# Normalising a linear-attention output: one Newton chain per batch instead of a power per block

## The chip, the cores and the metric

The kernel runs on one NeuronCore of one Trainium2 chip. Its time is the device time of one execution in microseconds (us), as the median of several runs. A profile is one further execution, recorded by the hardware profiler; its span runs from the first to the last instruction.

## The reference

Inputs are `q`, `k`, `v` of shape 8 batches x 8 heads x 576 tokens x 64, a gain `g_norm` of 64, and the weights of four experts. All are float32. The kernel computes

```python
kv  = einsum('bhsd,bhse->bhde', k, v)          # one 64x64 matrix per head
out = einsum('bhsd,bhde->bhse', q, kv)
rms = sqrt(mean(out * out, axis=-1, keepdims=True) + 1e-6)
x   = (out / rms * g_norm), heads side by side  # 576 x 512 per batch
logits = x @ w_gate                            # 4 experts, the best 2 are used
# per expert: causal softmax attention of x @ wq, x @ wk, x @ wv, then @ wo
# result: sum over the two chosen experts, weighted with a softmax of their logits
```

The norm is over the 64 numbers of one head and one token: 8 norms per token, 4608 per batch.

## The kernel before

The 576 tokens of a batch are five blocks, four of 128 and one of 64. Two generators per batch issue the work.

`stage1(b)` turns q, k, v into `xT`, the normalised x with its 512 features on the partitions. It adds up `kv` on TensorE (`p_kv`, line 175), transposes q block by block (`q_block`, lines 192 to 201) and puts `kv` times the router's weights behind each head's 64 columns (`p_kg`, lines 218 to 227), so that a head has 68 columns. Then, per block (lines 247 to 299): four matmuls give `p_out` with 8 x 68 columns in a "big" PSUM buffer (two banks); ACT squares its 64-column parts into `sq`; DVE sums them to `ms`, 8 numbers per token; GpSimd raises `ms` to the power -0.5 (`rstd`, line 268); DVE multiplies `p_out` with it into `x_tok` (line 273) and does the same for the router's part (`gl`, `lg8`). `x_flush` transposes `x_tok` on TensorE (`p_x`, line 242), one block behind, and ACT copies the result into `xT`.

`stage2(b)` makes the gate from `lg8`, the values `p_v`, and for each of two pairs of experts the projections (`p_proj`), the scores with their exponentials and masks (`p_sc`, `PT`; the masks are on GpSimd, line 394), the product with the values (`p_O`, scaled on DVE into `osc`) and its transposes (`p_OT`). `final` multiplies with `wo` (`p_y`), copies on ACT and writes out.

`weave` (lines 497 to 511) interleaves `stage2(b)` with `stage1(b + 1)`: each yields a cost, and the side work is advanced whenever its share of `W1` = 16 is behind the main work's share of `W2` = 17. A scheduler then settles the order on each engine, so the order that runs is not quite that in which the code issues; the excerpts below show it. There are three "big" PSUM buffers (for `p_out`, `p_proj`, `p_sc`, `p_O`) and two "small" ones (for the transposes, `p_kv`, `p_v`, `p_y`). Loads and stores are all issued from SP, in its order. The first `stage1` runs alone, the last `stage2` too, so seven pairs are woven.

Of the kernel before, what the change touches and what calls it, by code (L numbers as in the profile page):

```python
# [17 lines left out]
def kernel(  # L18
# [168 lines left out]
    def stage1(b, res):  # L187
        qb, kb, vb = loads[b]
        qT = s1.tile([P, NCH, S], FP32, tag="qT", name="qT")
# [44 lines left out]
        lg8 = lg8s[b % 2]  # L234
        pend = []

        def x_flush():
            i, xt = pend.pop(0)
            t0, nt = blocks[i]
            p_x = small([P, NCH, P], "p_x")  # L240
            for c in range(NCH):
                nc.tensor.transpose(  # L242
                    p_x[:, c, :nt], xt[:nt, c * P : (c + 1) * P], ident_f[:nt, :nt]
                )
            nc.scalar.copy(xT[:, :, t0 : t0 + nt], p_x[:, :, :nt])  # L245
# [310 lines left out]
```

## Time and profile before

| | before |
|---|---|
| runs, median (lowest to highest) | 370.99 us (370.33 to 371.15), 3 runs |
| the profiled execution | 370.28 us, span 368.6 us |
| TensorE busy, matmuls and weight loads | 298.2 us (81%) and 237.2 us (64%) |
| DVE, ACT, GpSimd (POOL) busy | 157.5, 152.6, 102.9 us |
| mean granted clock of TensorE | 0.852 of full speed |
| HBM read and written | 30.42 and 9.44 MB |

Busy time says what an engine did, and the chain of waits says what the end waited for. The chain is followed back from the last instruction, at each step to what released it. PE is TensorE's matmuls, PEld its weight loads, POOL is GpSimd. In the column of the clock 1.00 is full speed.

### The profile page before, as it was taken

The numbers are of one execution on the slowest core, as the hardware profiler recorded it, in microseconds if no ns is written. First come the engines' busy times: TensorE is split into PE (matmuls) and PEld (weight loads), VectorE is DVE, ScalarE is ACT, GpSimd is POOL, SyncE is SP. The second block draws the span as 40 slices with busy tenths as digits, with TensorE's granted clock in tenths as the row PEclk, the third lists the DMA queues.
The fourth block names the chain that finished last, engine by engine and source line by source line (L and its number), as shares of the span: only waits on it lengthen the run. The fifth ranks groups of instructions, "written<-read, shape, count | busy, mean of one in ns | idle before, by whom it ended". The sixth has DMA issues, their size and how long they took to land.

```text
span 368.6 us, 6665 instructions
## 1 busy us (share of the span) xinstructions
PE 298.2 (81%) x2616; PEld 237.2 (64%) x2624; DVE 157.5 (43%) x513; ACT 152.6 (41%) x273; POOL 102.9 (28%) x146
## 2 busy tenths in 40 slices
PE   2586698878986999779985899779995899778974
PEld 2474677668865788558864687557864687557651
DVE  0336443544436443544436433543444543544040
ACT  0213146132572347422582227621673227622843
POOL 8015113240253103530253103530235102521220
PEclk9978599578999599977999689986999589986975
DMA  7959999601136862900872035810021000300213
GB/s 216 211 128 291 278 232 293 123 4 57 58 115 160 129 202 56 246 12 19 239 198 61 2 123 152 212 29 2 0 88 43 2 2 0 130 1 2 85 44 128
DMA packets 75278, 40.28 MB, mean 109 GB/s; under 512 B 54000, under 2 KB 70384, under 8 KB 75248
## 3 DMA queue, kind: packets, MB, share of 16 engines
q1 hardware_dynamic: 75248, 39.86, 42.1%
q8 instruction: 21, 0.34, 0.4%
q14 instruction: 9, 0.07, 0.1%
HBM read 30.42 MB, written 9.44 MB: 108 GB/s over the span
## 4 chain that ended last, share of the span: by engine, by line
PE 46%; POOL 17%; DVE 17%; ACT 10%; issue 3%; SPq 2%; DMA 2%; POOLq 0%; ACTq 0%; DVEq 0%
POOL rstd L268 17%; PE p_proj L351 11%; PE p_v L333 7%; ACT PT L389 7%; DVE x_tok L273 7%; DVE ms L266 7%; PE p_kv L175 6%; PE p_out L250 5%; PE p_q L196 4%; PE p_sc L379 3%; PE p_x L242 2%; ACT sq L259 2%; PE p_kg L220 2%; SPq L130 2%; PE p_O L431 2%
## 5 line engine op out<-in xcount | busy, mean ns | idle before, releaser
L268 POOL TENSOR_TENSOR rstd<-ms,neg_half 128x8 f32<-128x8 f32 (+1 forms) x40 | 65.4, 1637 | 101.4 <-DVE ms L266 70.1
L394 POOL TENSOR_SCALAR_AFFINE_SELECT PT<-PT 128x256 bf16<-128x256 bf16 (+1 forms) x80 | 30.0, 385 | 148.8 <-ACT PT L389 148.1
L242 PE MATMUL p_x<-ident_f,x_tok 128*128 128x128 f32 (+1 forms) x160 | 30.7, 318 | 41.4 <-DVE gl L280 35.4
L250 PE MATMUL p_out<-kvx,qT 128*128 128x136 f32 (+1 forms) x320 | 55.1, 315 | 2.1 <-DVE inv L447 0.7
L389 ACT ACTIVATE PT<-p_sc 128x576 bf16<-128x576 f32 (+3 forms) x80 | 50.3, 712 | 7.2 <-PE p_sc L379 7.1
L250 PEld LDWEIGHTS p_out<-kvx,qT 128*128 128x128 f32 (+1 forms) x320 | 44.8, 197 | 11.5 <-issue 3.3
L273 DVE TENSOR_TENSOR x_tok<-p_out,rstd 128x512 f32<-128x512 f32 (+1 forms) x40 | 27.6, 690 | 55.0 <-POOL rstd L268 54.9
L242 PEld LDWEIGHTS p_x<-ident_f,x_tok 128*128 128x128 f32 (+1 forms) x160 | 19.2, 167 | 48.6 <-issue 34.4
L245 ACT CAST xT<-p_x 128x512 fp32r<-128x512 f32 (+1 forms) x40 | 21.7, 544 | 65.8 <-PE p_x L242 65.7
L259 ACT ACTIVATE sq<-p_out 128x512 f32<-128x512 f32 (+1 forms) x40 | 23.8, 596 | 47.9 <-PE p_out L250 47.0
L431 PE MATMUL p_O<-vext,PT 128*128 128x65 bf16 (+2 forms) x480 | 33.7, 211 | 7.3 <-DVE gl L280 5.1
L266 DVE TENSOR_REDUCE ms<-sq 128x8 f32<-128x520 f32 (+1 forms) x40 | 27.2, 680 | 26.9 <-ACT sq L259 26.9
L431 PEld LDWEIGHTS <-PT 128*128 128x128 bf16 (+2 forms) x480 | 27.8, 111 | 14.4 <-issue 9.7
L201 DVE COPY qT<-p_q 128x512 f32<-128x512 f32 (+1 forms) x40 | 25.4, 638 | 21.9 <-PE p_q L196 21.4
L333 PE MATMUL p_v<-wv_r,xT 128*128 128x256 f32 (+1 forms) x160 | 31.7, 335 | 0.3 <-DVE vext L340 0.3
L351 PE MATMUL p_proj<-xT,wq_r 128*128 128x288 f32 x128 | 31.4, 367 | 0.3 <-ACT PT L389 0.3
L175 PE MATMUL p_kv<-v_b,k_b 128*64 128x64 f32 x512 | 26.1, 263 | 5.7 <-DMA v_b<-in_v_dram 5.7
L379 PE MATMUL p_sc<-qTp,kT 64*128 64x288 f32 (+2 forms) x192 | 27.3, 345 | 2.0 <-ACT PT L389 1.7
L175 PEld LDWEIGHTS p_kv<-v_b,k_b 128*64 128x64 f32 x512 | 23.4, 176 | 8.0 <-DMA k_b<-in_k_dram 5.5
L196 PE MATMUL p_q<-ident_f,q_b 128*128 128x128 f32 (+1 forms) x160 | 26.0, 284 | 0.0
L333 PEld LDWEIGHTS p_v<-wv_r,xT 128*128 128x128 f32 (+1 forms) x160 | 24.5, 212 | 2.4 <-DVE vext L340 0.5
L340 DVE CAST vext<-p_v 128x256 bf16<-128x256 f32 (+1 forms) x40 | 17.0, 426 | 20.2 <-PE p_v L333 20.0
(61 smaller groups left out, 351.1 us busy)
## 6 DMA issues: line engine op xcount, KB each, us to landing
q_b<-in_q_dram SPq DMA_DIRECT2D x32, 256.0 KB, 5.2
out_dram<-y SPq DMA_DIRECT2D x32, 256.0 KB, 2.2
k_b<-in_k_dram SPq DMA_DIRECT2D x7, 1024.0 KB, 5.9
v_b<-in_v_dram SPq DMA_DIRECT2D x7, 1024.0 KB, 9.5
k_b<-in_k_dram SPq DMA_DIRECT2D x4, 256.0 KB, 4.5
v_b<-in_v_dram SPq DMA_DIRECT2D x4, 256.0 KB, 4.7
k_rem<-in_k_dram SPq DMA_DIRECT2D x8, 128.0 KB, 9.0
v_rem<-in_v_dram SPq DMA_DIRECT2D x8, 128.0 KB, 8.1
```

The source lines that it names most:

```text
L175: nc.tensor.matmul(p_kv[hh * Dh : (hh + 1) * Dh, c, :], lhsT=lk, rhs=rv, start=(j == 0), stop=(j == NF), skip_group_check=True,)
L196: nc.tensor.transpose(p_q[:, c, :nt], qb[:nt, i, 2 * c : 2 * c + 2, :].rearrange("p h d -> p (h d)"), ident_f[:nt, :nt],)
L242: nc.tensor.transpose(p_x[:, c, :nt], xt[:nt, c * P : (c + 1) * P], ident_f[:nt, :nt])
L250: nc.tensor.matmul(p_o[:nt, c // 2, (c % 2) * 2 * GW : (c % 2 + 1) * 2 * GW], lhsT=qT[:, c, t0 : t0 + nt], rhs=kvb[:, c, :, :].rearrange(" ...
L266: nc.vector.tensor_reduce(ms[:nt], sq[:nt], axis=AX_X, op=AluOpType.add)
L268: nc.gpsimd.tensor_tensor(out=rstd[:nt], in0=ms[:nt], in1=neg_half[:nt], op=AluOpType.pow)
L273: nc.vector.tensor_tensor(out=xt[:nt].rearrange("p (k h d) -> p k h d", k=2, h=4), in0=po[:, :, :, 0:Dh], in1=rb.to_broadcast([nt, 2, 4, Dh]),
L333: nc.tensor.matmul(p_v[:nt, :], lhsT=xT[:, c, t0 : t0 + nt], rhs=w_r["v"][:, c, :, :].rearrange("p e f -> p (e f)"), start=(c == 0), stop= ...
L351: nc.tensor.matmul(p_p[:, s, 0:HALF], lhsT=w_r[nm][:, c, 2 * pr : 2 * pr + 2, :].rearrange("p e f -> p (e f)"), rhs=xT[:, c, s * HALF : (s ...
L379: nc.tensor.matmul(p_s[:, el, o : o + hi - lo], lhsT=kTp[pb, kb * P : (kb + 1) * P], rhs=qTp[pb, lo:hi], start=True, stop=True,)
L389: nc.scalar.activation(PT[:, :, d0 : d0 + o], p_s[:, :, 0:o], ACTF.Exp, scale=scale)
L431: nc.tensor.matmul(p_O[:nq, bank, (2 * n + el) * (Hd + 1) : (2 * n + el + 1) * (Hd + 1)], lhsT=PT[:nk, el, col : col + nq], rhs=vx[:nk, kb ...
```

## The change

- After the four `p_out` matmuls of a block, DVE copies all 8 x 68 columns to a buffer in SBUF (`ob`, one for all batches); ACT then squares from PSUM as before and DVE sums into `ms[:, i, :]`, which now holds all five blocks.
- After the fifth block, DVE computes all 40 columns at once: an integer shift and a subtraction on the bits give a first value of 1/sqrt, and four Newton steps of three operations improve it. One multiply and one sum make the router's logits of the whole batch.
- The multiply that makes `x_tok` runs on GpSimd, from SBUF, five times in a row. `x_tok` has six buffers.
- The transposes `p_x` follow at the end, and `weave` holds the side work back by a new rule, with `W1` = 14 and `W2` = 14.3.
- To make room, the weights are staged in one buffer instead of two, `wo` in the same one, and `qT` has one buffer.

```diff
-    wst = ctx.enter_context(tc.tile_pool(name="wst", bufs=2))
+    wst = ctx.enter_context(tc.tile_pool(name="wst", bufs=1))
...
+        t = const.tile([P, NB, H], FP32, name=f"ms{j}")
+        nc.gpsimd.memset(t[REM:P, NF], 1.0)
+        mss.append(t)
+    ob = const.tile([P, NB, H, GW], FP32, name="o_sb")
+    nc.gpsimd.memset(ob[REM:P, NF], 0.0)
...
-    wo_st = wst.tile([P, EP, D], FP32, name="wo_st", tag="wo_st", bufs=1)
+    wo_st = wst.tile([P, EP, D], FP32, name="wo_st", tag="w_stage")
...
-        qT = s1.tile([P, NCH, S], FP32, tag="qT", name="qT")
+        qT = s1.tile([P, NCH, S], FP32, tag="qT", name="qT", bufs=1)
...
+            nc.vector.tensor_copy(
+                out=ob[:nt, i].rearrange("p (k h) g -> p k (h g)", k=2), in_=p_o[:nt, :, 0 : 4 * GW]
+            )
             sq = sqs[i % 3]
             nc.scalar.activation(
...
-            ms = blk.tile([P, H], FP32, tag="ms", name="ms")
-            nc.vector.tensor_reduce(ms[:nt], sq[:nt], axis=AX_X, op=AluOpType.add)
-            rstd = blk.tile([P, H], FP32, tag="rstd", name="rstd")
+            nc.vector.tensor_reduce(ms[:nt, i, :], sq[:nt], axis=AX_X, op=AluOpType.add)
+            yield 0.93
+
+
+        m = ms[:].rearrange("p n h -> p (n h)")
...
+        half = tiny("half", I32)
+        nc.vector.tensor_scalar(out=half[:], in0=m.bitcast(I32), scalar1=1, scalar2=None, op0=AluOpType.logical_shift_right)
+        y = tiny("y")
+        nc.vector.tensor_scalar(
+            out=y[:].bitcast(I32), in0=half[:], scalar1=-1.0, scalar2=float(0x5F3759DF),
+            op0=AluOpType.mult, op1=AluOpType.add,
+        )
+        for it in range(4):
+            u, w, y2 = tiny("u"), tiny("w"), tiny("y")
+            nc.vector.scalar_tensor_tensor(out=u[:], in0=y[:], scalar=0.5, in1=y[:], op0=AluOpType.mult, op1=AluOpType.mult)
+            nc.vector.tensor_tensor(out=w[:], in0=u[:], in1=m, op=AluOpType.mult)
+            nc.vector.scalar_tensor_tensor(out=y2[:], in0=w[:], scalar=1.5, in1=y[:], op0=AluOpType.subtract, op1=AluOpType.mult)
+            y = y2
+        gl = blk.tile([P, NB * H, E], FP32, tag="gl", name="gl")
...
+        xts = []
+        for i, (t0, nt) in enumerate(blocks):
+            xt = blk.tile([P, H, Dh], FP32, tag="x_tok", name="x_tok", bufs=NB + 1)
             nc.gpsimd.tensor_tensor(
-                out=rstd[:nt], in0=ms[:nt], in1=neg_half[:nt], op=AluOpType.pow
...
+                out=xt[:nt],
+                in0=ob[:nt, i, :, 0:Dh],
+                in1=y[:nt, i * H : (i + 1) * H].unsqueeze(2).to_broadcast([nt, H, Dh]),
                 op=AluOpType.mult,
             )
...
+            xts.append(xt)
+        yield 0.0
...
-    W1, W2 = 16.0, 17.0
+    W1, W2 = 14.0, 14.3
+    OUT_END = 11.6 / W1
+
+    def target(a):
+        if a < 0.92:
+            return min(a / 0.72, 1.0) * OUT_END
+        return 1.0
...
-            while live and s < a:
+            while live and s < target(a):
```

Lines of the changed kernel are some 14 to 17 higher: `p_out` is line 243, the copy 250, the sum 260, the Newton steps 279 to 281, the multiply on GpSimd 296, `p_x` 307, `p_v` 347, `p_proj` 365, `p_O` 445, `p_OT` 477.

GpSimd, one woven batch, before: one power per block, the first among the masks (`PT` is a pair's table of exponentials).

```order
L394 AFFINE_SELECT PT_1056<-PT_1056 128x2x128 x3
L268 TENSOR_TENSOR rstd_1097<-ms_1095,neg_half_92 128x8
L394 AFFINE_SELECT PT_1056<-PT_1056 128x2x128
L394 AFFINE_SELECT PT_1056<-PT_1056 64x2x64
L268 TENSOR_TENSOR rstd_1132<-ms_1130,neg_half_92 128x8
L268 TENSOR_TENSOR rstd_1171<-ms_1169,neg_half_92 128x8
L268 TENSOR_TENSOR rstd_1228<-ms_1226,neg_half_92 128x8
L268 TENSOR_TENSOR rstd_1277<-ms_1275,neg_half_92 64x8
```

GpSimd, the same place in the changed kernel (`y` is the last Newton step's result).

```order
L408 AFFINE_SELECT PT_1093<-PT_1093 64x2x64
L296 TENSOR_TENSOR x_tok_1263<-o_sb_120,y_1256 128x512
L296 TENSOR_TENSOR x_tok_1265<-o_sb_120,y_1256 128x512
L296 TENSOR_TENSOR x_tok_1267<-o_sb_120,y_1256 128x512
L296 TENSOR_TENSOR x_tok_1269<-o_sb_120,y_1256 128x512
L296 TENSOR_TENSOR x_tok_1271<-o_sb_120,y_1256 64x512
```

All five multiplies now read one `y` and stand in a row behind all masks.

DVE, between the sum of block 4 and the gate, in the changed kernel (`inv` and `osc` scale the attention's result of a pair; before, these lines stood between single blocks' `ms`, `x_tok` and `gl`).

```order
L260 TENSOR_REDUCE ms0_104<-sq1_124 64x8
L461 TENSOR_TENSOR inv_1176<-inv_1176,gate_892 64x2
L460 RECIPROCAL inv_1292<-p_O_1291 128x2
L465 TENSOR_TENSOR osc_1177<-p_O_1175,inv_1176 64x128
L271 TENSOR_SCALAR half_1232<-ms0_104 128x40
L461 TENSOR_TENSOR inv_1292<-inv_1292,gate_892 128x2
L273 TENSOR_SCALAR y_1234<-half_1232 128x40
L465 TENSOR_TENSOR osc_1293<-p_O_1291,inv_1292 128x128
L279 SCALAR_TENSOR_TENSOR u_1236<-y_1234 128x40
L460 RECIPROCAL inv_1292<-p_O_1291 64x2
L280 TENSOR_TENSOR w_1237<-u_1236,ms0_104 128x40
```

The first Newton operations stand among the attention's last; the other nine follow with nothing between them.

TensorE, the end of a woven batch, before.

```order
L351 MATMUL p_proj<-xT,wq_r 128x288
L463 LDWEIGHTS osc
L463 MATMUL p_OT<-ident_b,osc 128x128
L463 LDWEIGHTS osc
L463 MATMUL p_OT<-ident_b,osc 128x128
L463 LDWEIGHTS osc
L463 MATMUL p_OT<-ident_b,osc 128x128
L242 MATMUL p_x<-ident_f,x_tok 128x64 x4
L351 MATMUL p_proj<-xT,wk_r 128x288
```

TensorE, the end of a woven batch in the changed kernel. Ahead of the first row stand all `p_O`, the first three blocks' `p_x` (a row of 12) and four of these `p_OT`.

```order
L477 LDWEIGHTS osc
L477 MATMUL p_OT<-ident_b,osc 128x64
L307 MATMUL p_x<-ident_f,x_tok 128x128 x4
L365 MATMUL p_proj<-xT,wq_r 128x288
L307 MATMUL p_x<-ident_f,x_tok 128x64 x4
L365 MATMUL p_proj<-xT,wk_r 128x288
L347 MATMUL p_v<-wv_r,xT 128x256 x4
L179 MATMUL p_kv<-v_b,k_b 64x64 x8
```

Before, the transposes of four blocks stood between the `p_out` and `p_O` matmuls; now all five stand behind them, and only five `p_OT` and one projection lie between.

## Rows read from the trace of the kernel before

**Rows 1.** The page, chain of waits by line, shares of the span.

```profile
POOL rstd L268 17%; PE p_proj L351 11%; PE p_v L333 7%; ACT PT L389 7%; DVE x_tok L273 7%; DVE ms L266 7%; PE p_kv L175 6%; PE p_out L250 5%; PE p_q L196 4%; PE p_sc L379 3%; PE p_x L242 2%; ACT sq L259 2%; PE p_kg L220 2%; SPq L130 2%; PE p_O L431 2%
```

**Rows 2.** The chain in order of time: start us, length us, what.

```profile
179.91 1.19 PE p_proj L351 x8
...
212.40 3.70 PE p_kv L175 x80
...
223.05 1.19 PE p_proj L351 x8
224.23 0.79 PE p_kg L220 x8
...
250.54 0.66 PE p_x L242 x4
...
251.74 0.13 PE p_OT L463
...
254.55 3.17 PE p_kv L175 x80
...
264.66 1.19 PE p_proj L351 x8
```

**Rows 3.** TensorE's waits in 223:265: us in total, times, longest.

```profile
PE p_x L242 <- DVE gl L280: 4.7, 4, 2.1
```

**Rows 4.** Windows: length, busy us (instructions) of each engine, clock, DMA share, GB/s.

```profile
253.00:256.00 3.00, 3.00 (x34) 2.38 (x35) 0.80 (x4) 0.64 (x1) 0.00 (x0) 0.50 0.02 5
256.00:259.00 3.00, 3.00 (x68) 2.85 (x64) 0.97 (x3) 0.69 (x2) 0.00 (x0) 1.00 0.00 0
```

**Rows 5.** TensorE's timeline in the same batch: start us, length us, instruction.

```profile
231.00 1.09 PE L250 MATMUL p_out<-kvx,qT 128*128 128x136 f32 x8
231.92 1.03 PE L487 MATMUL p_y<-wo_b,OT 128*128 128x512 bf16 x4
232.79 0.63 PE L250 MATMUL p_out<-kvx,qT 128*128 128x136 f32 x4
...
235.60 0.53 PE L431 MATMUL p_O<-vext,PT 128*128 128x65 bf16 x12
```

**Rows 6.** Groups by line, whole span: busy us, mean ns | idle before, releasers.

```profile
L266 DVE TENSOR_REDUCE ms<-sq 128x8 f32<-128x520 f32 (+1 forms) x40 | 27.2, 680 | 26.9 <-ACT sq L259 26.9
L259 ACT ACTIVATE sq<-p_out 128x512 f32<-128x512 f32 (+1 forms) x40 | 23.8, 596 | 47.9 <-PE p_out L250 47.0 <-DVE ms L266 0.8
L214 DVE COPY kvT<-p_kt 128x512 f32<-128x512 f32 x8 | 5.5, 692 | 5.5 <-PE p_kt L212 5.5
```

**Rows 7.** DVE's timeline in the same batch.

```profile
238.75 0.56 DVE L451 TENSOR_TENSOR osc<-p_O,inv 128x384 bf16<-128x384 f32 x1
...
250.32 0.17 DVE L280 TENSOR_TENSOR gl<-p_out,rstd 64x32 f32<-64x32 f32 x1
...
251.29 0.28 DVE L451 TENSOR_TENSOR osc<-p_O,inv 64x128 bf16<-64x128 f32 x1
...
253.46 0.19 DVE L325 RECIPROCAL rden<-den 128x5 f32<-128x5 f32 x1
253.69 0.18 DVE L327 TENSOR_TENSOR gate<-gt,rden 128x20 f32<-128x20 f32 x1
```

**Rows 8.** GpSimd's groups by line, shapes apart, whole span.

```profile
L268 POOL TENSOR_TENSOR rstd<-ms,neg_half 128x8 f32<-128x8 f32 x32 | 52.4, 1638 | 68.8 <-DVE ms L266 40.5 <-DVE inv L447 12.5 <-DVE lg L286 9.4
...
L86 POOL MEMSET kv<- 128x512 f32 x2 | 1.1, 530 | 0.0
...
L89 POOL MEMSET lg<- 128x40 f32 x2 | 0.3, 132 | 0.0
```

**Rows 9.** Timeline of DVE and SP's queue in the first batch.

```profile
23.41 0.75 DVE L155 TENSOR_SCALAR wv_r<-w_stage,g_wide 128x1024 fp32r<-128x1024 f32 x1
...
40.27 0.68 DVE L273 TENSOR_TENSOR x_tok<-p_out,rstd 64x512 f32<-64x512 f32 x1 [1.49 <-POOL rstd L268]
...
24.19 2.02 SPq L154 DMA_DIRECT2D w_stage<-in_moe_wk_dram  x4
```

More of the change, by code (lines that the diff above doesn't have):

```diff
@@ L12 @@
 BF16 = mybir.dt.bfloat16
+I32 = mybir.dt.int32
 ACTF = mybir.ActivationFunctionType
@@ L71 @@
     make_identity(nc, ident_b[:])
-    neg_half = const.tile([P, H], FP32, name="neg_half")
-    nc.gpsimd.memset(neg_half[:], -0.5)
-    kr, vr, kvx, kv2s, sqs, lg8s, kTs, vexts = [], [], [], [], [], [], [], []
+    kr, vr, kvx, kv2s, sqs, lg8s, kTs, vexts, mss = [], [], [], [], [], [], [], [], []
     for j in range(2):
@@ L233, in stage1 @@
         xT = s1.tile([P, NCH, S], FP32R, tag="xT", name="xT")
[L234 to L245, printed above, removed]
+        lg8, ms = lg8s[b % 2], mss[b % 2]
         for i, (t0, nt) in enumerate(blocks):
@@ L260, in stage1 @@
                 sq[:nt, :, 0:Dh].rearrange("p (k h) d -> p k h d", k=2),
-                po[:, :, :, 0:Dh],
+                p_o[:nt, :, 0 : 4 * GW].rearrange("p k (h g) -> p k h g", g=GW)[:, :, :, 0:Dh],
                 ACTF.Square,
@@ L273, in stage1, with tiny @@
-            nc.vector.tensor_tensor(
-                out=xt[:nt].rearrange("p (k h d) -> p k h d", k=2, h=4),
-                in0=po[:, :, :, 0:Dh],
-                in1=rb.to_broadcast([nt, 2, 4, Dh]),
+            nc.vector.tensor_reduce(ms[:nt, i, :], sq[:nt], axis=AX_X, op=AluOpType.add)
+            yield 0.93
+        m = ms[:].rearrange("p n h -> p (n h)")
+        def tiny(name, dtype=FP32):
+            t = blk.tile([P, NB * H], dtype, tag=name, name=name)
+            return t
+        half = tiny("half", I32)
@@ new lines, in stage1 @@
+        gl = blk.tile([P, NB * H, E], FP32, tag="gl", name="gl")
+        nc.vector.tensor_tensor(
+            out=gl[:],
+            in0=ob[:].rearrange("p n h g -> p (n h) g")[:, :, Dh:GW],
+            in1=y[:].unsqueeze(2).to_broadcast([P, NB * H, E]),
+            op=AluOpType.mult,
+        )
+        nc.vector.tensor_reduce(
+            lg8[:, :, 0:E], gl[:].rearrange("p (n h) e -> p n e h", n=NB), axis=AX_X, op=AluOpType.add
+        )
+        xts = []
+        for i, (t0, nt) in enumerate(blocks):
+            xt = blk.tile([P, H, Dh], FP32, tag="x_tok", name="x_tok", bufs=NB + 1)
+            nc.gpsimd.tensor_tensor(
+                out=xt[:nt],
+                in0=ob[:nt, i, :, 0:Dh],
+                in1=y[:nt, i * H : (i + 1) * H].unsqueeze(2).to_broadcast([nt, H, Dh]),
@@ L277, in stage1 @@
                 op=AluOpType.mult,
             )
-            gl = blk.tile([P, H, E], FP32, tag="gl", name="gl")
-            nc.vector.tensor_tensor(
-                out=gl[:nt].rearrange("p (k h) e -> p k h e", k=2),
-                in0=po[:, :, :, Dh:GW],
-                in1=rb.to_broadcast([nt, 2, 4, E]),
-                op=AluOpType.mult,
-            )
-            nc.vector.tensor_reduce(
-                lg8[:nt, i, 0:E],
-                gl[:nt].rearrange("p h e -> p e h"),
-                axis=AX_X,
-                op=AluOpType.add,
-            )
@@ L292, in stage1 @@
-            pend.append((i, xt))
-            yield 0.9
-            if len(pend) > 1:
-                x_flush()
-                yield 0.45
-        while pend:
-            x_flush()
+            xts.append(xt)
+        yield 0.0
+        for i, (t0, nt) in enumerate(blocks):
+            p_x = small([P, NCH, P], "p_x")
+            for c in range(NCH):
+                nc.tensor.transpose(
+                    p_x[:, c, :nt],
+                    xts[i][:nt, 2 * c : 2 * c + 2, :].rearrange("p h d -> p (h d)"),
+                    ident_f[:nt, :nt],
+                )
+            nc.scalar.copy(xT[:, :, t0 : t0 + nt], p_x[:, :, :nt])
```

4 lines of the change are left out of this document (removed).

## The prediction

> **What bounds the kernel now.** I read the chain of waits first. Its largest single item is GpSimd's `rstd`, with 17% of the span, and `x_tok` and `ms` beside it have about 7% each [rows 1]. The reader is to see that an operation on 8 numbers per row outweighs every matmul line. The chain in order of time then shows one steady batch. It runs from the query projection of the second pair of experts at 223.05 to the same instruction of the next batch at 264.66, which is 41.61 us. The last x transposes (`p_x`) start at 250.54, 27.49 us into the batch, and 14.12 us are left after them [rows 2]. In the waits of TensorE for that stretch nearly all is `p_x`, 4.7 us in 4 waits, none over 2.1 [rows 3]. So each of the five token blocks goes once round ACT square, DVE sum, GpSimd power and DVE multiply, and the next block's `p_out` stands behind the transposes that wait for it. The windows show the clock: behind the idle time it is still at 0.50 in 253:256, though TensorE is busy for all of it, and at 1.00 again in 256:259 [rows 4]; of the two levels of 1.2 and 2.4 GHz the former is the 0.50.
>
> **The sum for one woven batch.** There are seven of them. I follow the new order from the same start, 0 = 223.05.
>
> *To the last `p_out`.* Before, TensorE went with hardly a gap from 0 to 9.74 (232.79, the start of block 2's `p_out`) [rows 2, 5]. That stretch holds the 16 projections, 12 of 20 q transposes, all scores of this pair, two `p_out` blocks, eight of ten output matmuls and the four `p_kg`. The last now stand ahead of the start, so 0.79 goes [rows 2]: 8.95. Behind come three more `p_out` blocks at 0.92 to 1.09, say 2.9, two output matmuls, about 0.4, and the first twelve `p_O` at 0.53 [rows 5]: 12.8. Three PSUM buffers serve `p_out`, scores and `p_O`. A block now keeps its buffer for a copy (0.69, as `kvT`, the same shape from PSUM) and a square (0.60) one after the other, instead of up to the multiply. For waits on these I add 0.3: 13.1.
>
> *From there to the sum of squares of block 4.* On DVE the copy stands behind the first heads' scaling: 0.7. Copy 0.69 and square 0.60 follow. The sum (0.68) stands behind the second pair's scaling, which waits for 30 `p_O` and takes about 1.1 with its reciprocals and products (its largest piece alone is 0.56) [rows 6, 7]. Together 3.75: 16.85.
>
> *Newton.* Of the 14 small operations five lie among eight of the attention's own. The trace has such a mixture at 0.11 apart (ten starts from 250.32 to 251.29) and operations that need each other at 0.23 (253.46 to 253.69) [rows 7]. I take 13 at 0.13 and 9 at 0.22, 3.7, and 0.15 for the hand-over to GpSimd: 20.7.
>
> *Five multiplies on GpSimd.* No row shows a 128x512 multiply there. The nearest below is a memset of that size, 0.53, which only writes; the nearest above is the same instruction kind with a power, 1.64 [rows 8]. Memsets of 40 and 512 elements (132 and 530 ns) give 0.84 ns per element and 0.10 of start. Two reads and one write make 0.96 where the write hides behind the reads, 1.39 where it does not. I take the middle, **1.17**, as the estimate; it lies nearer the upper row because there are two inputs. Five are 5.85, and `p_x` of block 4 stands at 26.6. Only the first multiply's latency is hidden: behind block 4's `p_out` TensorE has 48 `p_O` and five transposes, which end at about 17.3. So it waits 4.6 us in one piece up to 21.9, and then about 0.5 in front of each later block. That is a little more idle time than the 4.7 before, not less. For hand-overs and for small DVE work that gets in GpSimd's way I add 0.5: 27.1.
>
> *The rest.* After the last `p_x` stands the same work as before, 14.12, plus the `p_kg` moved here (0.79), less two transposes of 0.13 that now come earlier [rows 2]: 14.65. Together **41.75 against 41.61**, 0.14 more per batch, 1.0 for seven.
>
> **The first batch and the loads.** DVE's `wv_r` ends at 24.16 [rows 9]. After it come five copies, five sums and `wq_r`, 7.6, then 14 dependent operations, 3.1, and five multiplies, 5.85, with 0.4 for hand-overs: 41.3. Before, the last `x_tok` ended at 40.95 [rows 9]: 0.35 more. With one staging buffer the `wq` transfers leave once `wv_r` is done, where before those of `wk` left at 24.19 [rows 9]. At the 2.02 that four such issues take [rows 9], and as much again to land, they are in by 28.5, and `wq_r` has its turn on DVE behind five copies and three sums at 29.7, so its wait is hidden. The `wk` transfers wait for `wq_r`, and the remainder rows and q of batch 1 stand behind them on SP, so these leave at about 32.5 instead of 26.3. Their first reader, the `p_kv` of batch 1, stands behind the transposes that end at 41.3, and I cost this at nothing; where 9 us don't cover it, it costs what is lacking, 1 to 3 us once. The single `qT` buffer costs nothing: its last reader, block 4's `p_out`, is long done when the next copy is due. The last batch has no side work, so the end is unchanged.
>
> The sum is 1.0 + 0.35 on the profiled execution's 370.28, or 371.6. The runs' median is 0.7 above that execution, so I forecast **372.3**. About 0.2%, or 0.74 us, is what can be told from no change, so this is "slower" only by a little. Seventeen per cent of the chain goes, and five multiplies with one Newton chain take its place.
>
> **Rivals.**
> *The multiply is cheap (faster).* If the write hides wholly, 0.96 holds. Eight times five multiplies lose 0.21 each, 8.4 us: **364**. For it speaks the slope of the memset rows, against it that all other two-input prices here are unknown. Each 0.1 on the multiply is worth 4 us, so the sign turns at 1.14. Chance 0.28.
>
> *The clock comes back later (slower).* The wait becomes one of 4.6 us, and what follows the last `p_x` is one projection and four `p_v` before the 64-wide `p_kv`, where before five more projections stood in front of it. The trace shows what lateness costs: `p_kv` took 3.70 in the batch at 212 and 3.17 in the one at 254 [rows 2], and the batch around the former took 43.14, from 179.91 to 223.05 [rows 2], 1.5 us longer. If all seven run like that, they cost 10.5: **383**. Against it: the clock was at 0.50 in this place already. It decides where the clock is still 0.50 at the end of `p_kv`. Chance 0.14.
>
> *DVE and GpSimd hold each other up (slower).* While the multiplies run, DVE has five operations with two inputs in SBUF: `gl`, `sh`, `mk`, `gt` and `gate`. If each makes a multiply wait for its length, 0.18 for four [rows 7] and about 0.3 for the larger `gl`, and each hand-over costs another 0.1, the chain of multiplies grows by 1.5, of which 0.5 stands in the sum. Eight times 1.0 are 8: **380**. No row of before has such a pair at once. The Trainium skill (SBUF — State Buffer, "SBUF: two separate sides") says that the two engines share a pair of ports under an exclusive lock, and that the one that starts second waits for the whole instruction. No run here shows it yet. By that rule this rival is what happens, in part or in whole. Chance 0.14.
>
> The Trainium skill (GPSIMD Engine Reference, "Performance versus the Vector engine") also speaks against the change. It has elementwise arithmetic on GpSimd at about half VectorE's speed, with 4497 ns for 2048 fp32 elements; a quarter of that, an estimate, is 1.12, and the sum by it would come out about 2 us lower.
>
> **How the numbers follow.** My forecast's own case has a chance of 0.44. It covers 366 to 377, since the legs from the last `p_out` to the first multiply are good to about 0.7 us per batch, and it splits into 0.20 slower, 0.13 within 0.74 us and 0.11 faster. With the rivals that makes faster 0.39, same 0.13, slower 0.48. The price 0.53 would give 347, and 1.64 would give 391; I hold both ends unlikely, since two inputs must be read and a power is no multiply. The range of 8 in 10 goes from 362, a little below the cheap multiply, to 382, short of the worst clock.
>
> **What would show it.** Right: no `rstd` left; five `x_tok` rows on GpSimd in a row, 1.1 to 1.25 each; TensorE's `p_x` waiting once for 4 to 5 us and then four times for about 0.5; `p_x` of block 4 at some 27 us into the batch. The cheap multiply shows as `x_tok` under 1.0, the clock as 0.50 through the whole of `p_kv`, the hold-up as `x_tok` rows of unequal length or gaps between them. I am wrong altogether if `p_x` ceases to be TensorE's largest wait, or if the batch's end is set by another engine than GpSimd.

## The result and the profile after

| | before | after |
|---|---|---|
| runs, median (lowest to highest) | 370.91 us (370.33 to 371.15), 4 runs | 362.02 us (360.64 to 362.53), 4 runs |
| ratio of after to before | | 0.9757, 95% interval 0.9727 to 0.9786 |
| the profiled execution | 370.28 us, span 368.6 us | 362.53 us, span 360.7 us |
| TensorE, matmuls and weight loads | 298.2 and 237.2 us | 291.8 and 234.8 us |
| DVE, ACT, GpSimd busy | 157.5, 152.6, 102.9 us | 188.2, 153.0, 80.4 us |
| mean granted clock of TensorE | 0.852 | 0.837 |

The change makes the kernel 2.4% faster; the forecast was 372.3 us, slightly slower. The measured time stands at the lower end of its range. Ratios and intervals use fast runs alone: one run of e1_mult_on_dve below, at 350.74 us, counts as slow and is in its median and range but not in its ratio.

The page's chain of waits by line answers to [rows 1]. GpSimd's 17% has become 4%, and `p_x`, then 2%, is 10%. Another 22% is "issue" on the page, time for which the profile shows no releaser: in each batch 9.9 us of it stand ahead of the first multiply, where DVE ends the sums and the scaling and then runs the Newton steps.

```profile
PE p_proj L365 11%; PE p_x L307 10%; PE p_v L347 7%; PE p_kv L179 7%; PE p_q L200 5%; PE p_out L243 5%; ACT PT L403 4%; POOL x_tok L296 4%; PE p_sc L393 4%; PE p_kg L224 2%; PE p_y L501 2%; DVE o_sb L250 2%; DMA v_b<-in_v_dram 1%; POOL PT L408 1%; ACT y L506 1%
```

One steady batch in the chain in order of time (start us, us, what) answers to [rows 2]. It runs from 218.54 to 259.52, 40.98 us.

```profile
218.54 1.26 PE p_proj L365 x8
...
229.71 9.89 issue
239.65 1.19 POOL x_tok L296
...
240.88 3.17 PE p_x L307 x12
...
246.12 0.62 PE p_x L307 x4
...
248.13 3.41 PE p_kv L179 x80
...
252.21 0.66 PE p_proj L365 x5
...
259.52 1.26 PE p_proj L365 x8
```

TensorE's waits in 218:260 (us in total, times, longest), and its timeline at the one long wait, answer to [rows 3]: one piece of 4.3 us in place of four. The weight loads of TensorE (PEld), which come ahead of the matmuls, wait three times.

```profile
PE p_x L307 <- POOL x_tok L296: 4.3, 1, 4.3
PEld p_x L307 <- POOL x_tok L296: 5.0, 3, 4.4
```

```profile
240.88 3.15 PE L307 MATMUL p_x<-ident_f,x_tok 128*128 128x128 f32 x12 [4.30 <-POOL x_tok L296]
243.82 0.80 PE L477 MATMUL p_OT<-ident_b,osc 128*128 128x128 bf16 x5
244.79 1.09 PE L307 MATMUL p_x<-ident_f,x_tok 128*128 128x128 f32 x4 [0.18 <-ACT xT L312]
245.53 0.59 PE L365 MATMUL p_proj<-xT,wq_r 128*128 128x288 f32 x1
246.05 0.69 PE L307 MATMUL p_x<-ident_f,x_tok 64*128 64x64 f32 x4
```

```profile
241.88 0.72 PEld L307 LDWEIGHTS p_x<-ident_f,x_tok 128*128 128x128 f32 x4 [0.28 <-POOL x_tok L296]
242.91 0.72 PEld L307 LDWEIGHTS p_x<-ident_f,x_tok 128*128 128x128 f32 x4 [0.32 <-POOL x_tok L296]
```

The windows of that stretch, with the columns of [rows 4]: the granted clock is 0.50 through 247:250, the lower of the two levels of 1.2 and 2.4 GHz, with TensorE busy for all of it, and 0.96 in the next.

```profile
247.00:250.00 3.00, 3.00 (x41) 2.78 (x42) 0.43 (x1) 0.15 (x1) 0.00 (x0) 0.50 0.02 5
250.00:252.00 2.00, 2.00 (x54) 1.93 (x51) 0.41 (x1) 0.00 (x0) 0.00 (x0) 0.96 0.00 0
```

GpSimd's and DVE's groups, shapes apart (busy us, mean ns of one). The multiply, for which [rows 8] had no row, takes 1095 ns; three of DVE's gate operations, one of which took 0.18 us in [rows 7], take 525 to 959 ns.

```profile
L296 POOL TENSOR_TENSOR x_tok<-o_sb,y 128x512 f32<-128x512 f32 x32 | 34.2, 1095 | 96.7 <-DVE y L281 96.7
...
L329 DVE TENSOR_TENSOR sh<-lg,m 128x20 f32<-128x20 f32 x8 | 7.7, 959 | 0.3
L335 DVE TENSOR_TENSOR gt<-ex,mk 128x20 f32<-128x20 f32 x8 | 5.7, 709 | 3.0 <-ACT ex L331 3.0
...
L341 DVE TENSOR_TENSOR gate<-gt,rden 128x20 f32<-128x20 f32 x8 | 4.2, 525 | 0.3
```

The timelines of GpSimd, DVE and ACT at the same place:

```profile
239.65 5.21 POOL L296 TENSOR_TENSOR x_tok<-o_sb,y 128x512 f32<-128x512 f32 x5 [9.93 <-DVE y L281]
```

```profile
240.90 0.96 DVE L329 TENSOR_TENSOR sh<-lg,m 128x20 f32<-128x20 f32 x1
241.78 0.17 DVE L333 TENSOR_TENSOR mk<-lg,m 128x20 f32<-128x20 f32 x1
242.15 0.74 DVE L335 TENSOR_TENSOR gt<-ex,mk 128x20 f32<-128x20 f32 x1 [0.20 <-ACT ex L331]
```

```profile
241.89 0.22 ACT L331 ACTIVATE ex<-sh 128x20 f32<-128x20 f32 x1 [4.65 <-DVE sh L329]
242.03 0.58 ACT L312 CAST xT<-p_x 128x512 fp32r<-128x512 f32 x1
```

The multiplies end at 244.86, but block 4's `p_x` starts only at 246.05. The first three blocks still follow the multiplies: the weight loads of the second and the third wait 0.28 and 0.32 us for them, which the row of twelve matmuls does not show. Behind the third block TensorE sets the pace, at half clock: five `p_OT`, a wait of 0.18 for an ACT copy, block 3's transposes and a projection stand ahead of block 4's.

**Where the 7.9 us of span went.** The first woven batch starts at 55.05 where it started at 54.55: 0.5 lost. From there to the seventh start is 300.49 - 55.05 = 245.44 us, before 306.25 - 54.55 = 251.70: 6.26 won in six periods (40.91 each, before 41.95). What follows takes 60.21 us, before 62.35: 2.14 won. Of the 6.26, 4.9 lie ahead of the last `p_x` (27.34 us from a batch's start in the mean, before 28.15) and 1.4 behind it (13.56, before 13.80).

### The profile page after: what moved, and what is told of

It is laid out like the page before. It is cut to its first block, busy times and chain, and to the rows that moved or that the text cites. A ratio compares the mean times of both kernels' runs of the same rounds, so it can differ in the third digit from the quotient of the medians.

```text
span 360.7 us, 6721 instructions
## 1 busy us (share of the span) xinstructions
PE 291.8 (81%) x2616; PEld 234.8 (65%) x2624; DVE 188.2 (52%) x561; ACT 153.0 (42%) x273; POOL 80.4 (22%) x148
## 4 chain that ended last, share of the span: by engine, by line
PE 56%; issue 22%; ACT 9%; POOL 5%; DVE 4%; DMA 1%; SPq 1%; DVEq 0%; ACTq 0%; POOLq 0%
PE p_proj L365 11%; PE p_x L307 10%; PE p_v L347 7%; PE p_kv L179 7%; PE p_q L200 5%; PE p_out L243 5%; ACT PT L403 4%; POOL x_tok L296 4%; PE p_sc L393 4%; PE p_kg L224 2%; PE p_y L501 2%; DVE o_sb L250 2%; DMA v_b<-in_v_dram 1%; POOL PT L408 1%; ACT y L506 1%
## 5 line engine op out<-in xcount | busy, mean ns | idle before, releaser
L307 PE MATMUL p_x<-ident_f,x_tok 128*128 128x128 f32 (+1 forms) x160 | 39.2, 411 | 39.2 <-POOL x_tok L296 38.1
L296 POOL TENSOR_TENSOR x_tok<-o_sb,y 128x512 f32<-128x512 f32 (+1 forms) x40 | 42.1, 1083 | 96.7 <-DVE y L281 96.7
L307 PEld LDWEIGHTS p_x<-ident_f,x_tok 128*128 128x128 f32 (+1 forms) x160 | 26.9, 216 | 48.5 <-POOL x_tok L296 45.3
L243 PE MATMUL p_out<-kvx,qT 128*128 128x136 f32 (+1 forms) x320 | 45.8, 291 | 1.6 <-ACT PT L403 0.6
L243 PEld LDWEIGHTS p_out<-kvx,qT 128*128 128x128 f32 (+1 forms) x320 | 38.9, 182 | 6.3 <-ACT PT L403 3.3
L205 DVE COPY qT<-p_q 128x512 f32<-128x512 f32 (+1 forms) x40 | 24.8, 637 | 27.7 <-PE p_q L200 27.7
L254 ACT ACTIVATE sq<-p_out 128x512 f32<-128x512 f32 (+1 forms) x40 | 23.8, 595 | 27.8 <-DVE o_sb L250 19.2
L250 DVE COPY o_sb<-p_out 128x544 f32<-128x544 f32 (+1 forms) x40 | 28.8, 720 | 12.9 <-PE p_out L243 10.6
L260 DVE TENSOR_REDUCE ms<-sq 128x8 f32<-128x520 f32 (+1 forms) x40 | 27.3, 684 | 12.7 <-ACT sq L254 12.7
L445 PE MATMUL p_O<-vext,PT 128*128 128x65 bf16 (+2 forms) x480 | 29.1, 200 | 4.9 <-DVE osc L465 4.2
L445 PEld LDWEIGHTS <-PT 128*128 128x128 bf16 (+2 forms) x480 | 23.2, 103 | 13.8 <-issue 9.7
L179 PEld LDWEIGHTS p_kv<-v_b,k_b 128*64 128x64 f32 x512 | 25.2, 187 | 8.0 <-DMA k_b<-in_k_dram 4.5
L365 PE MATMUL p_proj<-xT,wq_r 128*128 128x288 f32 x128 | 25.7, 321 | 0.3 <-ACT PT L403 0.3
L501 PE MATMUL p_y<-wo_b,OT 128*128 128x512 bf16 (+1 forms) x72 | 23.4, 409 | 1.8 <-ACT OT L482 1.4
## 6 DMA issues: line engine op xcount, KB each, us to landing
q_b<-in_q_dram SPq DMA_DIRECT2D x32, 256.0 KB, 4.7
out_dram<-y SPq DMA_DIRECT2D x32, 256.0 KB, 2.0
k_b<-in_k_dram SPq DMA_DIRECT2D x4, 256.0 KB, 4.2
v_b<-in_v_dram SPq DMA_DIRECT2D x4, 256.0 KB, 4.5
```

Source lines behind the costliest of these rows:

```text
L179: nc.tensor.matmul(p_kv[hh * Dh : (hh + 1) * Dh, c, :], lhsT=lk, rhs=rv, start=(j == 0), stop=(j == NF), skip_group_check=True,)
L243: nc.tensor.matmul(p_o[:nt, c // 2, (c % 2) * 2 * GW : (c % 2 + 1) * 2 * GW], lhsT=qT[:, c, t0 : t0 + nt], rhs=kvb[:, c, :, :].rearrange(" ...
L250: nc.vector.tensor_copy(out=ob[:nt, i].rearrange("p (k h) g -> p k (h g)", k=2), in_=p_o[:nt, :, 0 : 4 * GW])
L296: nc.gpsimd.tensor_tensor(out=xt[:nt], in0=ob[:nt, i, :, 0:Dh], in1=y[:nt, i * H : (i + 1) * H].unsqueeze(2).to_broadcast([nt, H, Dh]), op ...
L307: nc.tensor.transpose(p_x[:, c, :nt], xts[i][:nt, 2 * c : 2 * c + 2, :].rearrange("p h d -> p (h d)"), ident_f[:nt, :nt],)
L365: nc.tensor.matmul(p_p[:, s, 0:HALF], lhsT=w_r[nm][:, c, 2 * pr : 2 * pr + 2, :].rearrange("p e f -> p (e f)"), rhs=xT[:, c, s * HALF : (s ...
```

## The experiments

All are compared with the kernel before, at 370.4 to 370.7 us in their runs. To read them I cut each woven batch of the profiled execution in two **legs**: from the start of the second pair's query projection, as in the chain, to the start of block 4's `p_x` on TensorE's timeline, and from there to the next such projection. In the row above these are 246.05 - 218.54 = 27.51 and 259.52 - 246.05 = 13.47.

| kernel | median us | leg to the last `p_x` | leg after it |
|---|---|---|---|
| before | 370.9 | 27.5 to 28.5 (29.5 once) | 13.6 to 14.7 (12.7 once) |
| after | 362.0 | 27.5 (26.5 once) | 13.5 (13.9 once) |
| e1_mult_on_dve | 348.0 | 26.0 to 26.8 | 11.8 and 13.7 by turns |
| e2_two_newton | 341.8 | 25.8 to 26.2 | 11.8 in four, 14.3 in two |
| e3_warm | 345.3 | 26.5, 27.0 in two | 11.8 |
| e4_old_weave | 365.3 | 28.9 to 29.2 (28.2 once) | 11.4 to 14.0 |
| e5_two_newton_dve | 337.0 | 24.6 to 25.3 | 11.7 to 13.8 |
| e6_two_newton_warm | 335.5 | 25.1 (26.1 once) | 11.8 (13.3 once) |
| e7_two_newton_dve_warm | 322.0 | 23.8 (23.4 once) | 11.8 |
| e8_before_warm | 358.5 | 28.0, 29.0 in two (28.3 once) | 11.7 (11.4 once) |
| e9_dve_warm | 334.0 | 25.2 (26.0 once) | 11.8 |
| e10_old_staging | 360.0 | 27.5 (26.5 and 27.0 once each) | 13.3 to 13.4 (11.8 and 14.3 once each) |
| e11_before_new_weave | 395.7 | 30.9 to 32.3 (27.7 once) | 13.9 to 15.2 |
| e12_first_on_dve | 370.2 | 28.8 (25.9 once) | 13.4 to 14.6 (12.7 once) |

My theory from the profile after, **C**: once the first `x_tok` is there, TensorE at half clock sets the pace. Its rival **G** is the prediction's own: GpSimd's five multiplies set the end. By the rows above neither holds for the whole row of blocks: the multiplies set the first three, TensorE the last two.

**e1_mult_on_dve**: the five multiplies on DVE, ahead of `gl`.

```diff
-            nc.gpsimd.tensor_tensor(
+            nc.vector.tensor_tensor(
```

> The five multiplies that make x_tok run on DVE instead of GpSimd, ahead of the router's multiply. Theory C (once the first x_tok is there, TensorE at half clock sets the pace, with some 1.0 us per block of transposes): the first x_tok comes 0.6 us earlier and the rest follows at TensorE's pace, so 0.6 x 8 = 5 us less, about 357 us. Theory G (GpSimd's five multiplies of 1.04 us set the end of the batch): 0.6 and another 5 x 0.4 less per batch, 2.6 x 8 = 21 us less, about 341 us. By both, the small DVE operations sh, gt and gate, which took 0.96, 0.71 and 0.53 us beside the multiplies on GpSimd, fall back to 0.17 to 0.18.

348.01 us (345.49 to 350.74), ratio 0.9366, interval 0.9315 to 0.9416: between the two. With a multiply now some 0.60 us behind the other on DVE, the first three blocks take 2.88 where they took 3.15: TensorE at half clock is faster than GpSimd's multiplies and slower than DVE's. The gate's operations are back at their old length, as the group below shows:

```profile
231.58 2.88 PE L307 MATMUL p_x<-ident_f,x_tok 128*128 128x128 f32 x12 [3.83 <-DVE x_tok L286]
```

```profile
L329 DVE TENSOR_TENSOR sh<-lg,m 128x20 f32<-128x20 f32 x8 | 1.4, 178 | 0.3
```

In the chain the `p_kv` of one batch and the next differ:

```profile
238.49 3.70 PE p_kv L179 x80
...
277.69 2.48 PE p_kv L179 x80
```

So the clock's return is a term of its own: where it is back before `p_kv`, the second leg is 1.9 shorter.

**e2_two_newton**: two Newton steps instead of four, 1.4 us less ahead of the first multiply.

```diff
-        for it in range(4):
+        for it in range(2):
```

> Two Newton steps instead of four, six dependent DVE operations of 0.23 us fewer. If the chain from block 4's sum to the first multiply is what TensorE waits for (both theories), every batch gets 1.4 us shorter: 8 x 1.4 = 11 us less, about 351 us. If TensorE's cold clock after the wait is what counts, the shorter wait may bring a little more (the clock comes back sooner), down to 347. If the end of the batch is set by something else, no change, 362.

341.77 us (340.66 to 344.15), ratio 0.9229, interval 0.9185 to 0.9272: 20 us for an edit worth 8 x 1.4 = 11. (Two steps leave a less exact 1/sqrt; how much less no run here measures.) The wait is 2.9 us instead of 4.3, and in four of six batches the clock is back with the last `p_x`:

```profile
230.00:232.00 2.00, 1.82 (x11) 1.46 (x11) 1.03 (x4) 1.66 (x4) 1.69 (x2) 0.50 0.00 0
232.00:234.00 2.00, 2.00 (x18) 1.61 (x18) 0.02 (x1) 1.03 (x3) 0.00 (x0) 0.96 0.00 0
```

**e3_warm**: TensorE gets unread matmuls for the time of the wait (`warm` is a constant tile; one ACT copy of `ms` into a column of it holds them back until the sums are there).

```diff
+            for n in range(20 if i == 0 else 0):
+                nc.tensor.matmul(
+                    p_x[:].rearrange("p c n -> p (c n)"), lhsT=ident_b[:], rhs=warm[:], start=True, stop=True
+                )
```

> Twenty matmuls of 128x512 bf16 that nobody reads run on TensorE in its wait for the first x_tok (they write the buffer of the first x transposes, which then overwrite it; a copy of one number on ACT makes them start behind block 4's sum). Theory C: the clock stays at 1.00 through the wait, the transposes take 0.6 instead of 1.0 us a block, so the last ones come when GpSimd is ready, 1.1 us earlier, and what follows them, 4.1 us at half clock, takes 2.0 less: 3 us per batch, 7 x 3 = 21 us less, about 341 us. Theory G: the clock costs nothing here, 362 us, or a little more if the extra matmuls run over the end of the wait.

345.33 us (344.25 to 345.49), ratio 0.931, interval 0.9282 to 0.9337: near C. With more work on TensorE the kernel is 16.7 us faster; `p_kv` takes 2.48 in every batch. At the full clock the matmul rows show waits for the multiplies too, 0.3 at a time (us, times, longest), and block 4's `p_x` starts 0.16 after the last multiply's end (153.13 + 5.21), where in the changed kernel it was 1.19:

```profile
PE p_x L314 <- POOL x_tok L299: 5.5, 16, 0.4
```

```profile
153.13 5.21 POOL L299 TENSOR_TENSOR x_tok<-o_sb,y 128x512 f32<-128x512 f32 x5 [9.94 <-DVE y L284]
```

```profile
158.50 0.46 PE L314 MATMUL p_x<-ident_f,x_tok 64*128 64x64 f32 x4
```

So at the full clock theory G holds for GpSimd's multiplies. In the two batches with 27.0 the unread matmuls ran partly at half clock and reached into the first transposes.

**e4_old_weave**: the weave's old constants and rule in the changed kernel.

```diff
-    W1, W2 = 14.0, 14.3
+    W1, W2 = 16.0, 17.0
...
-            while live and s < target(a):
+            while live and s < a:
```

> The changed kernel with the old rule and weights of the interleaving (16 and 17, no holding back). If the gain comes from the norms done at once, the place of the side work matters little: 362 to 365 us. If it comes from the new interleaving, most of it goes: 368 to 371 us.

365.29 us (363.08 to 367.67), ratio 0.9835, interval 0.9767 to 0.9902. Two runs are at 363.1 and two at 367.5, so the gain left over the kernel before is 1.0 to 2.3%. The new weave is worth 1 to 5 of the 9 us, 3 by the medians; the rest comes with the other edits. No run puts Newton steps in place of the power and leaves the rest, so what that edit is worth by itself is not shown. TensorE waits more for the attention's scaling, 13.8 us where the changed kernel has 4.1:

```profile
PE p_OT L477 <- DVE osc L465: 13.8, 14, 1.3
```

**e11_before_new_weave**: the other way round, the new weave alone in the kernel before.

```diff
-    W1, W2 = 16.0, 17.0
+    W1, W2 = 14.0, 14.3
...
-            while live and s < a:
+            while live and s < target(a):
```

> The kernel before the change, with the weave's new constants and target alone (the batch's x pieces keep their place in the stream, only the rate at which they are taken changes). e4_old_weave lost 3.3 of the 8.9 us when the weave was put back. If the two parts of the change add up: 370.7 - 3.3 = 367. If the new weave is of use only together with the batched norms, whose wait has to be reached early: 370 to 374, since the per-block waits come in one after the other with less other work between them.

395.68 us (392.92 to 396.80), ratio 1.0645, interval 1.0577 to 1.0713: 25 us slower, a miss in size. The parts do not add up. TensorE's waits say why:

```profile
PE p_proj L351 <- DVE m L308: 16.9, 6, 2.8
PE p_proj L351 <- DVE gl L280: 9.2, 6, 1.8
PE p_sc L379 <- DVE gl L280: 9.1, 7, 1.3
```

`p_proj` and `p_sc` share the three "big" PSUM buffers with `p_out`, and there a `p_out` keeps its buffer through square, sum, power and multiply up to `gl`. None of these waits on DVE is in the changed kernel's list, where the buffer goes after a copy (0.72) and a square (0.60). I read from this that the copy to SBUF lets `p_out` be taken early; no run has the copy alone.

**e8_before_warm**: the kernel before with four such matmuls in front of every block's transposes.

```diff
+            for n in range(4):
+                nc.tensor.matmul(
+                    p_x[:].rearrange("p c n -> p (c n)"), lhsT=ident_b[:], rhs=warm[:], start=True, stop=True
+                )
```

> The kernel before the change, with four unread 128x512 bf16 matmuls (0.85 us at full clock) in front of every block's x transposes, where TensorE waits 1.2 us at a time. It asks what the kernel before would be worth at the full clock, beside e3_warm (345.3), which is the change at the full clock. If the half clock costs the kernel before what it costs the changed one: the 5.5 us after the last p_x that run at 0.50 shrink by 2.7 a batch, seven times, 19 in all, so about 351, and the change is worth some 6 without the clock. If the loop through ACT, DVE and GpSimd sets the time whatever the clock is, or if the added matmuls run over into the transposes: 366 to 374, and the change's gain is for the most part the clock's.

358.47 us (355.81 to 360.13), ratio 0.9662, interval 0.9616 to 0.9707: between the two. The second leg falls to 11.7, the same as in every kernel at the full clock; the first stays at 28.0. So the half clock cost the kernel before some 2 us per batch, nearly all behind the last `p_x`, and the first leg, with its loop through ACT, DVE and GpSimd and now the added matmuls in it, did not get shorter. The added matmuls cost something themselves: two batches have 29.0, and the first woven batch starts at 56.94 where it started at 54.55, 4.5 in all. Beside e3_warm the change is worth 13.1 us at the full clock, or some 8.6 without those 4.5.

**e5_two_newton_dve, e6_two_newton_warm, e7_two_newton_dve_warm** are e2_two_newton with the multiplies on DVE, with 10 unread matmuls, and with both (8 of them).

```diff
-        for it in range(4):
+        for it in range(2):
...
-            nc.gpsimd.tensor_tensor(
+            nc.vector.tensor_tensor(
...
+            for n in range(8 if i == 0 else 0):
```

> Both earlier edits together: two Newton steps, and the five multiplies on DVE ahead of gl. The first x_tok then comes 0.5 us earlier (0.68 for 1.19), the fifth 2.5 us earlier (five at 0.68 for 1.19 and four at 1.04). Theory C (after the first x_tok TensorE at half clock sets the pace): only the 0.5 counts, 4 us over eight batches, and the two batches of e2_two_newton whose p_kv was still at half clock gain some 2.7 each: 341.8 - 4 - 5 = about 332. Theory G (the multiplies set the end of the batch): 2.5 - 0.5 more per batch, so about 317. A third case, that the clock falls and comes back as in e2_two_newton in every batch, so that only the 0.5 is won: 338.

336.95 us (336.39 to 337.06), ratio 0.9084, interval 0.9069 to 0.9099: the third case, 338. The 4.8 us below e2_two_newton are what the earlier first `x_tok` is worth by that case.

> Two Newton steps, multiplies on GpSimd, and 10 unread 128x512 bf16 matmuls (2.1 us at full clock) in front of block 0's transposes, which fill most of the 2.9 us for which TensorE waits in e2_two_newton. If the half clock is what is left there: the granted clock stays near 1.00 in all batches, p_x goes to the multiplies' pace of 1.04 per block, the last p_x comes about 0.6 earlier, the two batches with a cold p_kv gain 2.7 each: about 331 to 333. If the clock had already given back what it can: 341, and slower than that if the added matmuls run over into the first transposes.

335.48 us (333.90 to 337.51), ratio 0.9051, interval 0.9003 to 0.9100: between; the profiled execution still has one batch with a leg of 13.3.

> Two Newton steps, multiplies on DVE, and 8 unread 128x512 matmuls in front of block 0's transposes. At full clock TensorE needs some 0.5 per block, so that the multiplies set the pace in both kernels: against e6_two_newton_warm the fifth x_tok comes 2 us earlier per batch. If the multiplies set the end once the clock is up: 15 us below e6_two_newton_warm, about 317. If something behind them does (ACT's copies of p_x at 0.54 per block, or gl, sh and gate on DVE, which the multiplies now push back by 3.4): 325 to 332.

321.97 us (320.33 to 322.66), ratio 0.8678, interval 0.8649 to 0.8707: 13.5 below e6_two_newton_warm, between the two cases. The leg falls from 25.08 to 23.79, by 1.29, though the fifth multiply ends 2.2 earlier in the batch. In e6_two_newton_warm block 4's `p_x` starts 0.17 after the last multiply's end (187.66 and 187.49); here it starts 1.05 after it (217.80 and 216.75), and the weight loads wait for ACT's copies twice a batch. So at the full clock GpSimd's multiplies set the leg, and DVE's no longer do. It is the fastest kernel of the study, 13% below the one before.

```profile
213.66 3.09 DVE L289 TENSOR_TENSOR x_tok<-o_sb,y 128x512 f32<-128x512 f32 x5
```

```profile
214.41 1.99 PE L314 MATMUL p_x<-ident_f,x_tok 128*128 128x128 f32 x12 [0.95 <-DVE x_tok L289]
...
217.80 0.46 PE L314 MATMUL p_x<-ident_f,x_tok 64*128 64x64 f32 x4
```

```profile
PEld p_x L314 <- ACT xT L319: 4.4, 16, 0.5
```

**e9_dve_warm**: e1_mult_on_dve with 16 unread matmuls, all four Newton steps.

```diff
-            nc.gpsimd.tensor_tensor(
+            nc.vector.tensor_tensor(
...
+            for n in range(16 if i == 0 else 0):
```

> All four Newton steps, multiplies on DVE, and 16 unread 128x512 matmuls in front of block 0's transposes: what the change is worth at the full clock with the multiplies on DVE, and the missing corner between e3_warm (345.3), e7_two_newton_dve_warm (322.0) and e6_two_newton_warm (335.5). If at the full clock the terms of the sum simply add up: two Newton steps are 1.4 per batch, as 26.48 to 25.08 to the last p_x in e3_warm and e6_two_newton_warm, eight times 11, so 333; the leg to the last p_x 25.2, the one after it 11.8. If they do not (something behind DVE, such as gl, sh and gate, is the bound of e7_two_newton_dve_warm): 322 to 328.

333.95 us (333.39 to 335.01), ratio 0.8997, interval 0.8947 to 0.9047, with a leg of 25.2: as expected. At the full clock the terms add up. Two Newton steps are 1.40 per batch with the multiplies on GpSimd (26.48 to 25.08) and 1.40 with them on DVE (25.19 to 23.79); the engine is worth 1.29 with four steps (26.48 to 25.19) and 1.29 with two. At half clock the same edits gave 20 and 14 us alone and 25 together.

**e10_old_staging**: two staging buffers again.

```diff
-    wst = ctx.enter_context(tc.tile_pool(name="wst", bufs=1))
+    wst = ctx.enter_context(tc.tile_pool(name="wst", bufs=2))
...
-            xt = blk.tile([P, H, Dh], FP32, tag="x_tok", name="x_tok", bufs=NB + 1)
+            xt = blk.tile([P, H, Dh], FP32, tag="x_tok", name="x_tok", bufs=NB)
```

> The change with two staging buffers for the weights as before (wo stays in them; x_tok and gl get one buffer less each to make room, which nobody waits for). The prediction costs the single buffer at nothing. By that: 362.0, with the first woven batch starting at 55.05 as now. If the later loads of batch 1 are what makes the first start 0.5 later than before the change: 54.5 and 361.5, or up to 3 us less where the p_kv of batch 1 waits for them.

360.00 us (358.80 to 360.45), ratio 0.969, interval 0.9638 to 0.9743, 2 us below the changed kernel's median. The first woven batch does not start earlier (55.65, against 55.05), so the later loads alone do not explain it; in the profiled execution one batch has legs of 27.0 and 11.8, because the clock came back early there. Inconclusive about the 2 us. In the changed kernel's first batch the last multiply ends at 41.52, where before it was 40.95; that is about the 0.5 at the start. The five take 5.66 there and 5.21 later, and the fourth (1.49 instead of 1.04) runs beside DVE's `wk_r`, which in e10_old_staging runs ahead of the Newton steps:

```profile
38.09 1.53 DVE L159 TENSOR_SCALAR wk_r<-w_stage,g_wide 128x1024 fp32r<-128x1024 f32 x1
```

```profile
35.86 5.66 POOL L296 TENSOR_TENSOR x_tok<-o_sb,y 128x512 f32<-128x512 f32 x5 [26.48 <-DVE y L281]
```

There the multiplies end at 43.70, 2.2 later, so no run shows the start with the old loads and all else as in the changed kernel.

**e12_first_on_dve**: only block 0's multiply on DVE.

```diff
-            nc.gpsimd.tensor_tensor(
+            (nc.vector if i == 0 else nc.gpsimd).tensor_tensor(
```

> The change with block 0's multiply alone on DVE (ahead of gl), the other four on GpSimd. Theory C (after the first x_tok TensorE at half clock sets the pace, 1.0 per block): only the first x_tok's 0.5 counts, and the clock comes back as in e1_mult_on_dve, so the time is that kernel's, 346 to 350. Theory G (the last multiply sets the end): four in place of five on GpSimd, 1.0 less in each of eight batches, 354. If DVE's multiply holds GpSimd's first one up for its whole length, only 0.35 is won per batch: 359.

370.20 us (369.13 to 371.30), ratio 0.998, interval 0.9954 to 1.0006: all of the gain is gone, against every case I gave. DVE, ACT and TensorE in one batch of it:

```profile
243.86 0.69 DVE L286 TENSOR_TENSOR x_tok<-o_sb,y 128x512 f32<-128x512 f32 x1
244.47 1.17 DVE L294 TENSOR_TENSOR gl<-o_sb,y 128x160 f32<-128x160 f32 x1
...
246.62 0.95 DVE L329 TENSOR_TENSOR sh<-lg,m 128x20 f32<-128x20 f32 x1
```

```profile
247.61 0.22 ACT L331 ACTIVATE ex<-sh 128x20 f32<-128x20 f32 x1 [6.09 <-DVE sh L329]
247.73 1.05 ACT L312 CAST xT<-p_x 128x512 fp32r<-128x512 f32 x2
```

```profile
248.44 1.08 PE L307 MATMUL p_x<-ident_f,x_tok 128*128 128x128 f32 x4 [1.80 <-ACT xT L312]
```

The GpSimd multiplies hold up `gl` (1.17, in the changed kernel 0.32) and `sh` (0.95, there 0.96), and `gl` stands behind DVE's own multiply. The gate's exponential `ex` waits for `sh`, and ACT runs it ahead of the copies `xT`: due when block 0's transposes end at about 245.8, these come behind `ex` at 247.73. There are two PSUM buffers for `p_x`, so TensorE waits 1.8 us for the third block. In the changed kernel `ex` leaves at 241.89, just in time for the first `xT`.

## Why the prediction was wrong

Its sum for a woven batch was 27.1 to the last `p_x` and 14.65 after it, 41.75 against 41.61. Measured were 27.51 and 13.47.

**The start of the leg was right.** From the batch's start at 218.54 the last `p_out` ends 13.5 in (forecast 13.1), block 4's sum 17.0 (16.85), and the first multiply starts 21.1 in (20.7). The wait is one piece of 4.3 us (4.6).

**"Five multiplies on GpSimd" had the size and half of the role.** The multiply takes 1.18 at first and then some 1.04, against 1.17; five end 26.3 in, against 26.6. But the forecast let block 4's `p_x` start there, 0.5 later with hand-overs, and had waits of 0.5 in front of each block. Two such waits are there, of 0.28 and 0.32, and `p_x` comes at 27.51. What it left out is that after 4.3 us of waiting TensorE is at half clock, so that the `p_OT`, transposes and projection behind the third block last longer than the multiplies. e3_warm shows it: at the full clock the leg is 26.5. So the half clock costs 1.0 here; the other misses of this leg hide part of it, and it came out 0.4 too short.

**"The rest" is the step that failed**, by 1.2 us per batch. I carried 14.12 over from one batch of before and added 0.53 of moved work. e8_before_warm shows what was in the 14.12: 11.71 us at the full clock and 2.4 of half clock. In the changed kernel the leg at the full clock is 11.81 (e3_warm), so of the 0.53 only 0.1 shows. In e8_before_warm 0.66 of the 11.71 are waits of the matmuls on ACT, and e3_warm has none in this leg; but one projection of it stands ahead of the last `p_x` there, so that how the 0.53 was made up for is not shown piece by piece. And the half clock costs 1.7, not 2.4. The trace shows the place. Five projections stood in front of `p_kv` before, at half clock; now they stand behind it at 252.21, at the full clock, and the clock is back 4.1 us after the last `p_x` (250.2, from 246.05), before 5.5 (256.0, from 250.54) [rows 2, 4]. That the clock can come back sooner I had weighed only as its opposite. Whether the changed order brings it back is not shown: in four other batches of before, which have the same order up to `p_kv`, it is back 4.3 to 6.7 us after the last `p_x`, and e1_mult_on_dve has it by turns early and late. Why it comes back when it does stays open.

**The base batch was a short one.** 41.61 was the shortest kind; the mean of six is 41.95, and the 43.14 that the rival on the clock quoted stands in the same [rows 2]. That is 2.0 us in six periods. Its first leg was short (27.49, in the mean 28.15) and its second long (14.12, in the mean 13.80): against the mean batch the change wins 0.8 in the first leg and 0.2 in the second, and "the rest" is 0.8 too long instead of 1.2. "The end unchanged" was wrong too: of the 2.14 won at the end, 1.0 is the seventh batch's leg to the last `p_x`, and 1.15 comes after it. And the changed kernel's median lies 0.5 below its profiled execution, where I added 0.7. The terms of the first batch add up to 41.1 and not to 41.3, so the 0.35 should have read 0.15; the last multiply ends at 41.52.

The sum of misses on the profiled execution, 362.53 against 371.6: six batches 6 x (41.75 - 40.91) = 5.0, the base 2.0, the end 2.3, less 0.15 at the start and 0.15 outside the span, together 9.0.

**The rivals.** *The cheap multiply* named the time, 364, but not the cause, so that the match is luck: 1.09 lies far nearer to 1.17 than to 0.96, and the row at 246.05 shows that at half clock the multiplies do not set the end. The Trainium skill's figure (GPSIMD Engine Reference, "Performance versus the Vector engine"), a quarter of which I gave as 1.12, was nearer than my 1.17; the trace has 1.095. *The clock comes back later* did not happen, but its price was real: filling the wait gives 16.7 us.

*DVE and GpSimd hold each other up* happened, and cost little here. On GpSimd the first multiply, beside `gl`, takes 1.18 instead of 1.04. For the rest it was DVE that waited: `sh` ends at 241.86 and `gt` at 242.89, 0.03 to 0.04 after the ends of the second and the third multiply (241.82 and 242.86). By the Trainium skill (SBUF — State Buffer, "SBUF: two separate sides") whichever of the two starts second waits for the whole instruction; the trace agrees for these two, and e1_mult_on_dve, with no GpSimd multiply, has `sh` at 178 ns. The forecast looked for the cost on GpSimd. It lies on what waits for DVE, and e12_first_on_dve shows it: 8 us, with the exponential in front of the copies.

**Of the signs it named**, the five rows in a line, one long wait and `p_x` as TensorE's largest wait came true; "four times for about 0.5" came as 0.28 and 0.32 on weight loads alone, four of the five rows were below the 1.1 it gave (1.03 to 1.07), and the batch's end was set by another engine than GpSimd, which it had named as being wrong altogether.
